# Delta-rule attention into a hard-swish MLP: the triangular substitution dealt out by shares, x's sums moved up one unit, the eleven-product form in four blocks

## The chip, the cores and the metric

One NeuronCore of a Trainium2 chip runs the whole program. The metric is device microseconds of one execution. The kernel before was timed three times: 685.58, 686.8 and 688.06 us, median 686.8 us. Line numbers below are those of the kernel before, which are also the ones in its profile.

## The reference, cut to what matters

```python
# q, k, v: (4, 8, 768, 48); beta: (4, 8, 768); w_in: (384, 2048); w_out: (2048, 384); all float32
k_n = k / (norm(k, axis=-1) + 1e-06)
for t in range(S):                      # a 48x48 state for each of the 4*8 (batch, head) pairs
    y[:, :, t] = einsum('bhd,bhde->bhe', q[:, :, t], state)
    v_old = einsum('bhde,bhd->bhe', state, k_n[:, :, t])
    state = state + beta[:, :, t] * einsum('bhd,bhe->bhde', k_n[:, :, t], v[:, :, t] - v_old)
x = y.transpose(0, 2, 1, 3).reshape(3072, 384)
h = x @ w_in
g = h * clip(h + 3, 0, 6) / 6
out = g @ w_out
```

## The kernel before, in words

**Attention.** The 768 tokens are cut into 24 steps of 32 tokens; a step holds the 4 batches on 4 x 32 partitions. Within a step the token-by-token recurrence is replaced by a unit lower-triangular system of 32 x 32 for each of the 32 (batch, head) pairs. Its inverse X is made ahead of time for a group of four steps at once, 128 problems on 128 partitions, by forward substitution on VectorE (`inverse`). That is one transposing move in (L456), then 30 rounds of a multiply (L746, `pr<-A`) and a subtract (L751, `A<-A,pr`) on 30 to 240 elements a partition, a memset (L755) and one transposing move out (L460). Group 0 is step 0, group g holds steps 4g-3 to 4g, and the last has three. `norms` makes the inverse lengths of a group's keys, two groups ahead: a square `sq<-kf` (L398) and a sum over it (L400) for each step, through one scratch tile.

`chain(t)` is the serial part of a step: the state times K and Q (L793, `ks`), two pairs of operations that build the right side R (L806, `R<-ks`), X times R (L814, `pz`), the state's update (L912 `su`, L928) and the output y (L806, L814 `py`, L849). Its last piece turns y on TensorE (L859, `yt`) and copies it into the MLP's input xT (L863). `prep(t)` makes what depends on K and Q alone, some steps ahead; GpSimd scales keys and masks for it (L497, L473, L485).

**MLP.** Two steps make a block of 256 rows, 12 blocks in all. `up(blk)` multiplies by w_in: 16 units, each with three matmuls of 128x128 by 256 columns into one buffer `ph` of the PSUM pool `psM`. That pool has four buffers, and `pt`, `py`, `pz`, `yt` and the down products take turns in the same ring. ScalarE (L976) and then VectorE (L979, `g<-g,ph`) evict each unit. For the last two blocks `up_by_eleven(blk)` does the same with 11 products of 128x128x128 in place of 12 for each of 8 pairs of columns of w_in (L1039). It needs sums of w_in's parts, made once on GpSimd (`weight_sums`, L1005), four differences of x's parts on VectorE (`token_sums`, L1029), three additions on GpSimd for each pair (L1005, `g<-g`), and three operations each on ScalarE (L1053, L1076, L1080) and VectorE (L1069, L1070, L1083) for each pair. `down_by_seven(blk)` multiplies by w_out with seven products in place of eight, with sums of g's parts (L1182) and of the outputs (L1206) on VectorE; its matmuls are L1196.

**Order.** Nothing is left to a scheduler. The first steps follow a list of words written by hand. From step 5 on, a loop deals every step out over 15 units. Each unit issues what `plan` has for it (pieces of `chain` and `prep`, loads), then one unit of the MLP (`units`, which runs through down and up of each block), then the evictions that are due, and last some of `fill`. `fill` is `norms` at first and then `inverse` of the next group; whatever is left of it is drained when the next group begins, since X is needed there. A block's `up` begins in unit 12 of an odd step and ends in unit 12 of the next, and `down_by_seven` takes the units up to unit 11 of the odd step after. The amount of `fill` in a unit, and where the sums of x stand, are in these lines:

```python
UF = 10                                                   # first block by eleven products
12: lambda: token_sums(t // CB) if t % CB and t // CB >= UF else None,
if i == 1 == ready[0] and 5 < u < 12:
    continue
take(fill, 1 if mode["slow"] else 2 + (u % 3 == 0))
```

`mode["slow"]` is set while `up_by_eleven` runs. In groups 3 to 5 the substitution for the next group begins in unit 6 of the group's second step, pauses to unit 11, and then goes at 3, 2 and 2 operations a unit.

Of the kernel before, what the change touches and what calls it, by code (L numbers as in the profile page):

```python
# [14 lines left out]
ACTF = mybir.ActivationFunctionType  # L15
# [31 lines left out]
def kernel(  # L47
# [21 lines left out]
    nc = tc.nc  # L69
# [321 lines left out]
    def norms(g, i0, n):  # L391

        kf = kfs[g]
        ss = small.tile([P, n, H], FP32, name="ss")
        for i in range(n):
            needs(("k", first(g) + i0 + i))
            sq = work.tile([P, H, D], FP32, name="sq", bufs=1)
            nc.scalar.activation(out=sq[:], in_=kf[:, i0 + i], func=ACTF.Square)  # L398
            yield 1
            nc.vector.tensor_reduce(out=ss[:, i, :], in_=sq[:], axis=AX.X, op=ALU.add)  # L400
            yield

        root = small.tile([P, n, H], FP32, name="root")
        nc.scalar.activation(out=root[:], in_=ss[:], func=ACTF.Sqrt, bias=tiny, scale=0.25)
        yield
        t = small.tile([P, n, H], FP32, name="nt")
        nc.vector.reciprocal(out=t[:], in_=root[:])
        yield
        nc.vector.scalar_tensor_tensor(
            out=t[:], in0=ss[:], scalar=0.25, in1=t[:], op0=ALU.mult, op1=ALU.mult  # L410
        )
        yield
        nc.vector.scalar_tensor_tensor(
            out=t[:], in0=t[:], scalar=1e-6, in1=root[:], op0=ALU.add, op1=ALU.add
        )
        yield
        inv = small.tile([P, n, H], FP32, name="inv", bufs=4)
        nc.vector.reciprocal(out=inv[:], in_=t[:])
        for i in range(n):
            invs[first(g) + i0 + i] = inv[:, i, :]  # L420
        yield
# [516 lines left out]
            yield  # L938


    mode = {"slow": False}
    gs, pos, evicts = {}, {}, []
    relus, pending = ({name: [] for name in ("a", "b", "u")} for _ in range(2))

# [45 lines left out]
                past.add(("up", blk))  # L990
            yield

    UF = 10
    S1, S2, S4 = (sums_in[:, i] for i in range(3))

    def w_tiles(s, i):
# [24 lines left out]
        return [x[:, s, i * P : i * P + P] for s in range(NKT) for i in range(CB)]  # L1021

    def token_sums(blk):
        needs(("seam", blk * CB), ("seam", blk * CB + 1), ("up", blk - 1))
        B11, B12, B21, B22, _, _ = (
            x.rearrange("p (a b) -> p a b", b=16) for x in x_tiles(blk)
        )
        for out, a, b in ((T1x, B12, B11), (T2x, B22, T1x), (B12, B22, B12), (T4x, B21, T2x)):
            nc.vector.tensor_tensor(out=out, in0=a, in1=b, op=ALU.subtract)  # L1029
        past.add(("sums", blk))  # L1030

    def up_by_eleven(blk):
        needs(("sums", blk))
        mode["slow"] = True
        B11, T3x, B21, B22, B31, B32 = x_tiles(blk)
        phs, ready = {}, {}

# [63 lines left out]
        for j in range(NPR):  # L1101
            end(j)
            go(j - 1)
            if j + 2 < NPR:
                yield
                begin(j + 2)
                go(j)
                yield
            else:
                go(j)  # L1110
                if j == NPR - 1:
                    go(j)
                    mode["slow"] = False
                yield

    def to_dram(t, o):
# [144 lines left out]
    def mlp_units():  # L1261


        u1 = up(1)
        for f in range(0, NFC, WF):
            for c in range(CB):
                down(0, c, f)
                yield
            for _ in range(WF):
                next(u1)  # L1270
                yield
        def downs(blk):
            if blk >= FIRST:
                yield from down_by_seven(blk)
                return
            for c in range(CB):
                for f in range(0, NFC, WF):
                    if c == 0:
                        needs(*(("read", ("ph", blk, f + i, None)) for i in range(2)))
                    down(blk, c, f)  # L1280
                    yield

        for blk in range(1, N // CB):
            sums = weight_sums() if blk == UF - 1 else iter(())
            for _ in downs(blk):
                next(sums, None)
                next(sums, None)
                yield
            if blk + 1 < N // CB:
                for n, _ in enumerate((up_by_eleven if blk + 1 >= UF else up)(blk + 1)):  # L1290
                    if blk + 1 == FIRST and n >= HF:
                        drain(rest)
                        if n % 2:
                            last_quarter(n - HF - 1)
                    yield
# [101 lines left out]
    with tc.manual_schedule():  # L1397
# [9 lines left out]
        units = gens["u"]  # L1407
        fill = inverse_of(2)
        loads = iter(())
        for t in range(LS, N):  # L1410
            g, i = group(t)
            ch = chain_of(t)
            behind = t - LS < LA - LE
            first_of = t + min(LA, LE + t - LS)
            now, more, later = (prep_of(first_of + n) for n in range(3))
            if not behind:
                more, later = (), more
            take(gens["v"], 4)
            if i == 0:
                drain(fill)  # L1420
                fill = norms_of(g + 2)
            if i == 2:
                loads = keys_of(g + 3)
            plan = {
                0: lambda: take(ch),
                1: lambda: (take(ch), take(now)),
                2: lambda: (take(now), take(gens["q"], 4)),
                3: lambda: take(ch),
                4: lambda: (take(ch), take(now)),
                5: lambda: take(now),  # L1430
                6: lambda: take(now),
                8: lambda: take(ch),
                9: lambda: take(ch, 2),
                11: lambda: take(ch),
                12: lambda: token_sums(t // CB) if t % CB and t // CB >= UF else None,
                13: lambda: take(later),
            }
            if behind:
                for u in (7, 8, 10, 11, 12, 13):
                    plan[u] = lambda ch=plan.get(u): (ch and u < 13 and ch(), take(more))  # L1440
                plan[14] = lambda: take(later)
            ready = (2, 0) if behind or i == 2 and t - LS == LA - LE else (1, 6)
            for u in range(NU):
                if u in plan:
                    plan[u]()
                take(loads, 2)
                if (i, u) == ready:
                    drain(fill)
                    fill = inverse_of(g + 1)
                    take(fill)  # L1450
                take(rest)
                take(gens["a"])
                take(units)
                settle(1)
                while evicts:
                    evicts.pop(0)()
                if i == 1 == ready[0] and 5 < u < 12:
                    continue
                take(fill, 1 if mode["slow"] else 2 + (u % 3 == 0))
            drain(ch)  # L1460
        for _ in units:
            settle(2)
# [30 lines left out]
```

## Time and profile before

| | |
|---|---|
| median of three runs | 686.8 us (685.58 to 688.06) |
| the profiled execution | 685.55 us, of which its span is 683.8 us |
| granted TensorE clock | 0.99 of full speed |
| TensorE busy | 647.7 us, 95% of the span |
| VectorE busy | 475.2 us, 69% |
| ScalarE, GpSimd busy | 253.3 us, 118.3 us |
| chain that ended last | TensorE 78%, VectorE 16%, issue 2%, ScalarE 2% |

The profile is one execution. Each matmul of float32 appears as two records, so 48 matmuls are 96 records. A row of the timeline reads: start in us from the span's start, the stretch in us, engine, line, operation, output and inputs, count, and in brackets how long the engine had stood idle and what ended that. Records overlap where an engine is pipelined, so a sum of durations is a little more than the time they take. In steps 9 to 16 a step takes about 26 us, in steps 17 to 21 about 24 us. The product with w_in of block 7 begins near 446 us, that of block 8 near 498, of block 9 near 546, of block 10 near 594 and of block 11 near 641.

### The profile page before, as it was taken

Reading aid. Unit: us, or ns where it says so; the run is one execution under the profiler, and the core shown is the slowest. Engines: PE = TensorE matmul, PEld = TensorE weight load, DVE = VectorE, ACT = ScalarE, POOL = GpSimd, SP = SyncE. Lnnn points to the kernel's source line nnn. Section 1 sums busy time; section 2 is a strip of 40 time slices with the busy share of each in tenths; the row PEclk is TensorE's granted clock in tenths of the full one; section 3 lists DMA queues with packets and bytes.
Section 4 is the critical chain, followed back from the end, with each engine's and each line's share of the span. In section 5 each row is a group of like instructions: output and inputs, shape, how many; then the busy total and the mean of one; then the engine's idle time right before and its main releaser. Section 6 shows DMA issues by size and latency. Waiting matters only on the chain.

```text
span 683.8 us, 25829 instructions
## 1 busy us (share of the span) xinstructions
PE 647.7 (95%) x11368; PEld 572.6 (84%) x11368; DVE 475.2 (69%) x1234; ACT 253.3 (37%) x503; POOL 118.3 (17%) x200
## 2 busy tenths in 40 slices
PE   2588989999999999999999999999999999999997
PEld 2468977776689989989988988978988989999997
DVE  5888867898556996746985746985546995457354
ACT  5986776423133133232133132132232132143250
POOL 6240232002311100100100101102000032040230
PEclk9997999999999999999999999999999999999999
DMA  7995435402040030041030030020020020100000
GB/s 182 246 215 132 99 88 130 80 4 45 23 86 14 3 72 2 3 89 19 2 71 2 3 71 2 2 61 2 3 47 2 3 48 2 28 11 2 25 1 23
DMA packets 88496, 33.23 MB, mean 49 GB/s; under 512 B 80160, under 2 KB 83232, under 8 KB 88384
## 3 DMA queue, kind: packets, MB, share of 16 engines
q1 hardware_dynamic: 88128, 31.29, 20.5%
q8 instruction: 89, 1.46, 0.9%
q10 hardware_dynamic: 256, 0.30, 0.2%
q14 instruction: 23, 0.19, 0.1%
HBM read 26.84 MB, written 4.72 MB: 46 GB/s over the span
## 4 chain that ended last, share of the span: by engine, by line
PE 78%; DVE 16%; issue 2%; ACT 2%; DMA 1%; SPq 0%; POOL 0%; DVEq 0%; ACTq 0%
PE ph L968 28%; PE po L1196 22%; PE ph L1039 6%; PE po L1131 4%; PE pt L513 3%; PE ks L793 3%; DVE g L1182 3%; PE py L814 3%; PE su L912 3%; PE pz L814 2%; DVE A L751 2%; DVE pr L746 2%; PE sc L534 2%; PE yt L859 1%; PE pi L671 1%
## 5 line engine op out<-in xcount | busy, mean ns | idle before, releaser
L968 PE MATMUL ph<-xT,w_in 128*128 128x256 f32 (+1 forms) x1056 | 227.4, 368 | 3.4 <-DVE g L979 2.8
L968 PEld LDWEIGHTS ph<-xT,w_in 128*128 128x128 f32 x1056 | 185.3, 194 | 27.7 <-DVE g L979 3.9
L976 ACT ACTIVATE g<-ph,halves 128x256 f32<-128x256 f32 (+1 forms) x176 | 79.1, 453 | 165.5 <-PE ph L968 163.4
L979 DVE SCALAR_TENSOR_TENSOR g<-g,ph 128x256 f32<-128x256 f32 (+1 forms) x176 | 68.1, 391 | 67.4 <-ACT g L976 67.2
L1196 PE MATMUL po<-w_out,g 128*128 128x192 f32 x640 | 112.1, 326 | 0.0
L1196 PEld LDWEIGHTS po<-w_out,g 128*128 128x128 f32 x640 | 104.7, 190 | 0.4
L1196 PE MATMUL po<-spare,g 128*128 128x192 f32 x480 | 86.7, 332 | 0.0
L1196 PEld LDWEIGHTS po<-spare,g 128*128 128x128 f32 x480 | 77.2, 190 | 1.8
L1182 DVE TENSOR_TENSOR g<-g 128x256 f32<-128x256 f32 x160 | 65.7, 459 | 3.3 <-PE po L1196 3.2
L473 POOL TENSOR_TENSOR mb<-beta_tok,mask 128x256 f32<-128x256 f32 x38 | 25.9, 702 | 236.8 <-DVE LB L545 236.8
L751 DVE TENSOR_TENSOR A<-A,pr 128x30 f32<-128x30 f32 (+9 forms) x150 | 53.7, 358 | 3.4
L746 DVE TENSOR_TENSOR pr<-A 128x30 f32<-128x30 f32 (+9 forms) x150 | 52.0, 347 | 3.1
L348 ACT ACTIVATE spare<-spare,places 128x768 uint16<-128x768 uint16 (+1 forms) x56 | 52.4, 940 | 2.9 <-DMA spare<-in_moe_w_in_dram 2.0
L1131 PE MATMUL po<-w_out,g 128*128 128x384 f32 x128 | 45.6, 493 | 0.0
L1203 ACT ACTIVATE o<-po 128x192 f32<-128x192 f32 x40 | 13.2, 330 | 82.4 <-PE po L1196 82.4
L521 ACT ACTIVATE KQ<-pt 128x512 f32<-128x512 f32 x48 | 28.1, 594 | 29.6 <-PE pt L513 29.2
L1039 PE MATMUL ph<-xT,w_in 128*128 128x128 f32 x224 | 34.2, 278 | 0.2
L497 POOL TENSOR_TENSOR kb<-kf,inv 128x384 f32<-128x384 f32 x24 | 22.3, 930 | 66.2 <-PE yt L859 35.6
L1131 PEld LDWEIGHTS po<-w_out,g 128*128 128x128 f32 x128 | 23.2, 190 | 12.4
L1005 POOL TENSOR_TENSOR g<-g 128x128 f32<-128x128 f32 x48 | 21.8, 455 | 67.8 <-ACT g L1053 65.3
L863 ACT ACTIVATE xT<-yt 128x384 f32<-128x384 f32 x24 | 11.7, 486 | 57.2 <-PE yt L859 57.2
L793 PEld LDWEIGHTS ks<-state,KQ 64*64 64x64 f32 x1472 | 24.8, 138 | 8.6 <-issue 7.7
(137 smaller groups left out, 779.7 us busy)
## 6 DMA issues: line engine op xcount, KB each, us to landing
kf<-in_k_dram SPq DMA_DIRECT2D x96, 48.0 KB, 2.7
qb<-in_q_dram SPq DMA_DIRECT2D x96, 48.0 KB, 2.9
vf<-in_v_dram SPq DMA_DIRECT2D x96, 48.0 KB, 2.1
out_dram<-o SPq DMA_DIRECT2D x92, 48.0 KB, 1.6
spare<-in_moe_w_in_dram SPq DMA_DIRECT2D x4, 768.0 KB, 7.6
w_out<-in_moe_w_in_dram SPq DMA_DIRECT2D x4, 768.0 KB, 7.1
w_out<-in_moe_w_out_dram SPq DMA_DIRECT2D x4, 768.0 KB, 6.6
spare<-in_moe_w_out_dram SPq DMA_DIRECT2D x4, 768.0 KB, 4.8
```

What stands on the lines that cost most here:

```text
L348: nc.scalar.activation(out=z, in_=z if n else d.bitcast(I16)[:, :, :, 3], func=func, bias=places[:, n : n + 1], scale=scale,)
L746: nc.vector.tensor_tensor(out=pv, in0=A[:, j + 1 :, j].unsqueeze(2).to_broadcast([n, w, j]), in1=A[:, j, 0:j].unsqueeze(1).to_broadcast([n ...
L751: nc.vector.tensor_tensor(out=A[:, j + 1 :, 0:j], in0=A[:, j + 1 :, 0:j], in1=pv, op=ALU.subtract)
L793: nc.tensor.matmul(ph[y][c, e, D * p : D * p + D], lhsT=KQ[r, p * B // 2 + b // 2, 2 * y : 2 * y + 2, :].rearrange("k y c -> k (y c)"), rh ...
L814: nc.tensor.matmul(ps[rows(place(b)), D * h : D * h + D], lhsT=m(h)[rows(b)], rhs=z[rows(b), D * h : D * h + D], start=True, stop=True, sk ...
L968: nc.tensor.matmul(ph[:, cols], lhsT=w_in[:, s, f * 128 : (f + 1) * 128], rhs=xT[:, s, cols], start=(s == 0), stop=(s == NKT - 1),)
L976: nc.scalar.activation(out=g, in_=ph, func=ACTF.Relu, bias=half, scale=1.0 / 6.0)
L979: nc.vector.scalar_tensor_tensor(out=g, in0=g, scalar=1.0, in1=ph, op0=ALU.min, op1=ALU.mult)
L1039: nc.tensor.matmul(ph[:, n], lhsT=w, rhs=x, start=start, stop=stop, skip_group_check=True)
L1131: nc.tensor.matmul(pos[c][:], lhsT=gs[blk, f // 2][:, f % 2, c * P : (c + 1) * P], rhs=w_out[:, f, :], start=(f == 0), stop=(f == NFC - 1),)
L1182: nc.vector.tensor_tensor(out=A(f, *out), in0=A(f, *a), in1=A(f, *b), op=op)
L1196: nc.tensor.matmul(ps[n][:], lhsT=A(f - f % 2, *a)[:, f % 2], rhs=b[:, f], start=(f == 0), stop=(f == HF - 1),)
```

## The change

Four edits. `UF` goes from 10 to 8, so that blocks 8 to 11 and not only 10 and 11 use `up_by_eleven`; `weight_sums` moves from block 9 to block 7 with it. `token_sums` moves from unit 12 to unit 11, right behind the chain's last piece and before that unit's part of the down product. The amount of `fill` while the substitution runs is no longer 3, 2, 2 a unit: what is left is divided by the units left in the group, and weighted by 0.9 beside `up`, 0.7 beside `up_by_eleven` and 1.25 beside `down`. The pause in the group's second step ends after unit 8, not 11. From group 4 on, the squares of `norms` are made by GpSimd and not by ScalarE.

```diff
@@ -395,7 +395,12 @@
         for i in range(n):
             needs(("k", first(g) + i0 + i))
             sq = work.tile([P, H, D], FP32, name="sq", bufs=1)
-            nc.scalar.activation(out=sq[:], in_=kf[:, i0 + i], func=ACTF.Square)
+            if g < 4:
+                nc.scalar.activation(out=sq[:], in_=kf[:, i0 + i], func=ACTF.Square)
+            else:
+                nc.gpsimd.tensor_tensor(
+                    out=sq[:], in0=kf[:, i0 + i], in1=kf[:, i0 + i], op=ALU.mult
+                )
             yield 1
             nc.vector.tensor_reduce(out=ss[:, i, :], in_=sq[:], axis=AX.X, op=ALU.add)
             yield
@@ -938,7 +943,7 @@
             yield
 
 
-    mode = {"slow": False}
+    mode = {"of": "down"}
     gs, pos, evicts = {}, {}, []
     relus, pending = ({name: [] for name in ("a", "b", "u")} for _ in range(2))
 
@@ -990,7 +995,7 @@
                 past.add(("up", blk))
             yield
 
-    UF = 10
+    UF = 8
     S1, S2, S4 = (sums_in[:, i] for i in range(3))
 
     def w_tiles(s, i):
@@ -1021,6 +1026,8 @@
         return [x[:, s, i * P : i * P + P] for s in range(NKT) for i in range(CB)]
 
     def token_sums(blk):
+        if blk < UF or ("seam", blk * CB + 1) not in past:
+            return
         needs(("seam", blk * CB), ("seam", blk * CB + 1), ("up", blk - 1))
         B11, B12, B21, B22, _, _ = (
             x.rearrange("p (a b) -> p a b", b=16) for x in x_tiles(blk)
@@ -1031,7 +1038,6 @@
 
     def up_by_eleven(blk):
         needs(("sums", blk))
-        mode["slow"] = True
         B11, T3x, B21, B22, B31, B32 = x_tiles(blk)
         phs, ready = {}, {}
 
@@ -1110,7 +1116,6 @@
                 go(j)
                 if j == NPR - 1:
                     go(j)
-                    mode["slow"] = False
                 yield
 
     def to_dram(t, o):
@@ -1281,12 +1286,14 @@
                     yield
 
         for blk in range(1, N // CB):
+            mode["of"] = "down"
             sums = weight_sums() if blk == UF - 1 else iter(())
             for _ in downs(blk):
                 next(sums, None)
                 next(sums, None)
                 yield
             if blk + 1 < N // CB:
+                mode["of"] = "eleven" if blk + 1 >= UF else "up"
                 for n, _ in enumerate((up_by_eleven if blk + 1 >= UF else up)(blk + 1)):
                     if blk + 1 == FIRST and n >= HF:
                         drain(rest)
@@ -1407,6 +1414,8 @@
         units = gens["u"]
         fill = inverse_of(2)
         loads = iter(())
+        left = due = 0
+        SHARE = {"up": 0.9, "eleven": 0.7, "down": 1.25}
         for t in range(LS, N):
             g, i = group(t)
             ch = chain_of(t)
@@ -1418,6 +1427,7 @@
             take(gens["v"], 4)
             if i == 0:
                 drain(fill)
+                left = 0
                 fill = norms_of(g + 2)
             if i == 2:
                 loads = keys_of(g + 3)
@@ -1431,8 +1441,7 @@
                 6: lambda: take(now),
                 8: lambda: take(ch),
                 9: lambda: take(ch, 2),
-                11: lambda: take(ch),
-                12: lambda: token_sums(t // CB) if t % CB and t // CB >= UF else None,
+                11: lambda: (take(ch), token_sums(t // CB)),
                 13: lambda: take(later),
             }
             if behind:
@@ -1448,15 +1457,21 @@
                     drain(fill)
                     fill = inverse_of(g + 1)
                     take(fill)
+                    left, due = 2 * (C - 2) + 2, 0.0
                 take(rest)
                 take(gens["a"])
                 take(units)
                 settle(1)
                 while evicts:
                     evicts.pop(0)()
-                if i == 1 == ready[0] and 5 < u < 12:
+                if i == 1 == ready[0] and 5 < u < 9:
                     continue
-                take(fill, 1 if mode["slow"] else 2 + (u % 3 == 0))
+                if not left:
+                    take(fill, 2)
+                    continue
+                due += SHARE[mode["of"]] * left / max((GS - i) * NU - u - 4, 1)
+                take(fill, int(due))
+                left, due = max(left - int(due), 0), due - int(due)
             drain(ch)
         for _ in units:
             settle(2)
```

## The prediction

> **What bounds the kernel now.** I read the page's busy times and slices first, then busy time by stretch, then the timeline where TensorE's matmuls start late.
>
> ```profile
> PE 647.7 (95%) x11368; PEld 572.6 (84%) x11368; DVE 475.2 (69%) x1234; ACT 253.3 (37%) x503; POOL 118.3 (17%) x200
> PE   2588989999999999999999999999999999999997
> DVE  5888867898556996746985746985546995457354
> ```
>
> TensorE is full from the ninth slice on. VectorE swings between 4 and 9 with a period of about six slices, the four steps of a group: its peaks are the substitution. So TensorE sets the time, and VectorE costs something only where a peak makes TensorE wait. I took the starts of all matmuls and looked for steps longer than the shape's usual one. From 200 us on, apart from 0.09 to 0.14 us whenever the kind of matmul changes, only these stand out: 1.00 us at 246.8, 0.32 at 339.8, 0.99 at 350.5, 0.31 at 443.6, 1.34 at 454.2, 0.91 at 594, 0.89 at 641. That is 5.8 us in all, the most that a better order can give there. The largest:
>
> ```profile
> 453.89 0.74 DVE L806 SCALAR_TENSOR_TENSOR R<-ks,parity,vf 128x192 f32<-128x192 f32 x2
> 454.55 0.73 DVE L806 SCALAR_TENSOR_TENSOR R<-ks,parity,R 128x192 f32<-128x192 f32 x2
> 455.19 0.41 DVE L979 SCALAR_TENSOR_TENSOR g<-g,ph 128x256 f32<-128x256 f32 x1
> 455.66 1.56 PE L968 MATMUL ph<-xT,w_in 128*128 128x256 f32 x6 [1.18 <-DVE g L979]
> ```
>
> The eviction `g` stands behind R, and R behind substitution operations: `ks` was done near 450.8 and R begins at 453.89. The two `pt` of a `prep` have taken two of the four buffers of the ring, so the next `ph` has to wait for that `g`. The stalls at 246.8 and 350.5 are alike; those at 339.8 and 443.6 are `yt` waiting for y. The last two are the sums of x:
>
> ```profile
> 594.08 0.35 DVE L1206 TENSOR_TENSOR o<-u,po 128x192 f32<-128x192 f32 x1 [1.06 <-PE po L1196]
> 594.36 0.28 DVE L1029 TENSOR_TENSOR beta_tok<-xT 128x128 f32<-128x128 f32 x1
> 594.79 0.46 PE L1039 MATMUL ph<-beta_tok,sums_in 128*128 128x128 f32 x2 [0.52 <-DVE beta_tok L1029]
> ```
>
> xT was written by 593.27, but the sums stand behind `o<-u,po`, which waits for the last down product.
>
> **Eleven products in blocks 8 and 9.** GpSimd's rows pace block 11's pairs, where hardly anything else runs; the ordinary product is read between two rows of TensorE:
>
> ```profile
> 652.07 1.53 POOL L1005 TENSOR_TENSOR g<-g 128x128 f32<-128x128 f32 x3 [0.93 <-ACT g L1053]
> 654.52 1.52 POOL L1005 TENSOR_TENSOR g<-g 128x128 f32<-128x128 f32 x3 [0.93 <-ACT g L1053]
> 656.98 1.53 POOL L1005 TENSOR_TENSOR g<-g 128x128 f32<-128x128 f32 x3 [0.93 <-ACT g L1053]
> 367.30 2.76 PE L968 MATMUL ph<-xT,w_in 128*128 128x256 f32 x12
> 369.90 2.76 PE L1196 MATMUL po<-w_out,g 128*128 128x192 f32 x16
> ```
>
> A pair takes (656.98 - 652.07)/2 = 2.455 us with eleven products. Twelve records, two units, take 369.90 - 367.30 = 2.60 us. So 0.145 us a pair, 8 pairs, two more blocks: -2.3 us on TensorE. `weight_sums` are the same 16 operations in an earlier block; GpSimd is busy 17% of the span and 4.2 of 24 us beside block 7's product, so I cost them at nothing. If they were late, block 8's first products would wait for them.
>
> **Sums of x a unit earlier.** In blocks 10 and 11 they then start right after xT, near 593.3, and the first is done before the second product of the pair wants it at about 594.1. Of 0.91 + 0.89 us I take back 1.6: -1.6. The `o` operations that move behind them have 7 us until ScalarE's L1080 (at 601.5) writes their tile again. In blocks 8 and 9 the sums are new.
>
> **Spreading the substitution.** In the built order I counted L746 and L751 between one step's y (L849) and the next. Groups 3 and 4 have 28 then 32 before (down, then up) and 32, 26 and 2 after. So six operations of about 0.38 us, 2.3 us of VectorE, leave the part beside `up`, where R and `g` were late by more than 1 us of their margin. Of 0.99 + 1.34 I expect 1.8 back. The part before y has four more, but they begin in unit 9 and not 12 and thin out toward y (2.5 a unit falling to 2.0, against 2.3), so y may be about 0.2 us earlier at each of the two `yt`: 0.4 back. Together -2.2; the bounds are -3.0 (all stalls gone) and 0 (they only move). Group 2 is the other way: 21 then 35 become 25 then 32, so y of step 7 is some 1.2 us later (four of 0.3). Its `yt` has no margin to speak of when VectorE is that full (the two stalls of 0.3 show it), and the 1.0 us at 246.8 shrinks a little: +0.5, between -1.0 and +1.2.
>
> **Squares on GpSimd.** At steps 5, 9 and 13 ScalarE squares and VectorE sums in turn, 1.14 us a round. GpSimd's `kb<-kf,inv` of the same 384 elements takes 0.83 to 1.0 us, so a round becomes about 1.5, but only two rounds instead of three precede R: R comes no later. ScalarE gets free for `KQ<-pt`, which was late at step 5, where TensorE lost 0.8 us before `sc` at 169.3: -0.5, between -0.8 and +0.5 (if GpSimd delays a `kb`).
>
> **Block 9: substitution beside eleven products.** This decides. Before, 27 operations of the last substitution stand beside block 9's product with w_in; after, 24, for the share of 0.7 takes out few when the deadline is near. The stretch before, and block 10 without substitution:
>
> ```profile
> core 0: us, PE busy (x) PEld busy (x) DVE busy (x) ACT busy (x) POOL busy (x), PEclk, DMA share, GB/s
> 546.00:570.00 24.00, 24.00 (x352) 20.55 (x351) 21.11 (x54) 7.97 (x17) 8.76 (x12) 1.00 0.16 36
> 594.00:618.00 24.00, 23.41 (x427) 22.49 (x426) 12.18 (x32) 11.46 (x23) 10.84 (x24) 1.00 0.11 26
> ```
>
> VectorE before: 21.1 us. Out go 16 `g` of 0.42 (6.7) and three substitution operations (about 1.2). In come 8 times 0.29 + 0.42 + 0.68 = 1.39 (11.1) and four sums of 0.29 (1.2): 25.5 us, against 24.0 - 1.2 = 22.8 of TensorE. It is over by 2.7. GpSimd adds to it:
>
> ```profile
> 439.14 1.03 POOL L485 TENSOR_TENSOR bkb<-kb,beta_tok 128x384 f32<-128x384 f32 x1 [3.46 <-PE su L912]
> 439.52 0.91 DVE L751 TENSOR_TENSOR A<-A,pr 128x234 f32<-128x234 f32 x1
> ```
>
> An `A<-A,pr` of this size takes 0.40 us elsewhere; it ends 0.3 us after GpSimd's. Six operations of VectorE are stretched so beside `weight_sums` between 551 and 561, 2.6 us in all, which the 21.1 contains; R and `g`, which read PSUM, are not stretched (0.73, 0.41 us). GpSimd now has 24 additions of 0.5 us, 12.1 for 8.8 us, so 2.6 may become 3.6: +1.0. And VectorE enters later, with four more operations beside block 8's down product (+1.4). The upper bound is 2.7 + 1.0 + 1.4 = 5.1 us. The lower is 0: VectorE may fall behind by a ring's depth, about one pair (2.5 us) or a little more, and catch up in the next down product, where it is busy 12.1 of 24 us. Before, that stretch lost nothing at 88% of VectorE. I take the middle, +2.7: about 1.2 of it where block 9's second product waits for the sums of x, the rest where a begun pair waits for a buffer. Block 8 has only five operations and the move in (1.97 us) beside its product: +0.3, between 0 and 1.
>
> The Trainium skill (SBUF — State Buffer, "Who interferes with whom") says that a VectorE instruction with two SBUF inputs and a GpSimd instruction that reads SBUF exclude each other, the second waiting until the first is done; the rows at 439 agree. By that rule alone, block 9's product would hold the port for 12.1 us of GpSimd, 8 of substitution, 5.5 of L1083 and 2 of other sums, 27.6 us for 22.8, so it speaks against the change: about +4.8 in place of +2.7, and about -1.0 for the whole.
>
> **Sum.** -2.3 - 1.6 - 2.2 + 0.5 - 0.5 + 2.7 + 0.3 = -3.1 us: the profiled 685.55 becomes 682.4. The median lies 1.25 above that execution, so the forecast is 686.8 - 3.1 = 683.7 us. A measurement of this kernel tells 0.3%, 2.1 us, from no change.
>
> **Rivals.** (a) Block 9 hides its load behind the ring as before: without the 2.7 and 0.3 the sum is -6.1, 680.7 us. For it: TensorE was at 24.00 of 24.00 us there. Against it: 25.5 us of VectorE in 22.8. (b) The spread only moves the stalls: VectorE has as much to do, and the later ends meet the next step's work. Then -2.2 becomes 0 and the sum is -0.9, 685.9, no change. For it: the operations beside `down` grow. (c) Slower. GpSimd and VectorE take turns in blocks 8 and 9: each substitution operation waits out a whole addition of 0.5 us, and GpSimd's delay holds up L1069 in turn. 24 + 5 operations times 0.5 are 14.5 us, of which some 4 fit into VectorE's idle time and 2.5 into the ring; with the 2.7 over and 1.4 late that is +12 in place of +3.0, so the sum is about +6, 692.8. It decides for slower once an operation waits more than 0.35 us on average ((3.1 + 2.1 us over what the forecast has) / 29 = 0.18, beside the 0.1 to 0.2 already in). Rows near 559 show 0.20 to 0.57 beside additions of 0.73, so half a wait of 0.5 is likelier. (d) The change not doing what it says: the built order shows all four edits, so only their effect is open.
>
> **How the numbers follow.** Forecast (681.8 to 685.5) 0.42, (a) 0.18, (b) 0.20, (c) in its whole width from +1.5 us 0.20. Faster by over 0.3% (below 684.7): 0.8 of the forecast's cases and all of (a), 0.52. Slower by over 0.3% (above 688.9): the upper two thirds of (c), 0.14, and 0.04 from unknowns, 0.18. Within: 0.30. The range leaves out the best part of (a) and the far part of (c): 680.3 to 689.0.
>
> **What would show it.** Right: no matmul of `ph` late by 1 us near 350 and 454; none behind the sums of x in blocks 10 and 11; blocks 8 and 9 with 2.455 us a pair where no chain piece lies between; a stall of 1 us or more at the start of block 9's product, with VectorE above 95% in it. Wrong: TensorE full through block 9 (then a), substitution rows of 0.7 us and more throughout block 9 with TensorE idle several us (then c), or `yt` and R late by as much as before (then b).

## The result and the profile after

The changed kernel takes 685.23 us (median of 20 runs, 681.46 to 689.79), the kernel before 688.0 us on the same chip (20 runs, 683.4 to 693.02). The ratio is 0.9958, 95% interval 0.9942 to 0.9974: about 2.8 us faster. The profiled execution after took 685.23 us with a span of 683.1. Line numbers after are those of before plus 5 to 7; a line is named here by its tiles too.

The page of after, busy times and two rows of slices:

```profile
PE 644.3 (94%) x11528; PEld 575.7 (84%) x11528; DVE 487.6 (71%) x1258; ACT 257.1 (38%) x508; POOL 150.3 (22%) x259
PE   2668989999999999999999999999999999999997
DVE  5878776888645996746986746987548998557364
```

TensorE has 3.4 us less to do and is still full from the ninth slice on. VectorE shows the same swing. Its last peak has nines in slices 32 and 33 as before, and the slices on both sides of them have gone from 6 and 5 to 8 and 8: blocks 8 and 9.

**Where the time went.** The first 155 us wait on loads and vary by themselves: the first `yt` of step 4 came at 154.39 us before, at 157.56 after, and between 153.9 and 158.9 in the runs below, whose instructions up to there do not differ. From then on a stretch whose instructions do not differ repeats to 0.05 us from profile to profile, with one exception: step 20 of the two versions below with an early last group, -0.38 and -0.57. For this reason all differences below are taken between first `yt` records in the trace: "step 7" runs from the first `yt` of step 6 to that of step 7, and "to the end" is the last matmul's end. There is one profile of each kernel. Each kernel against the kernel before, in us:

| steps | 5 | 7, 8 | 11, 12 | 15, 16 | 18, 19 | 20, 21 | 22 to the end | all from step 5 |
|---|---|---|---|---|---|---|---|---|
| the changed kernel | -0.30 | +0.83 | -1.29 | -1.64 | +0.12 | +0.42 | -2.10 | -3.96 |
| dealing-out alone | -0.51 | +0.82 | -1.29 | -1.64 | 0.00 | 0.00 | -0.01 | -2.65 |
| eleven in blocks 8, 9 alone | -0.02 | -0.02 | -0.02 | -0.02 | +0.31 | +4.24 | -0.01 | +4.46 |
| sums of x alone | -0.02 | -0.02 | -0.02 | -0.03 | 0.00 | 0.00 | -2.09 | -2.18 |
| squares on GpSimd alone | +0.49 | -0.03 | -0.02 | -0.38 | 0.00 | 0.00 | -0.01 | +0.07 |
| all but eleven in blocks 8, 9 | -0.33 | +0.80 | -1.29 | -1.63 | 0.00 | 0.00 | -2.10 | -4.55 |

**The stalls.** After 200 us four places of the changed kernel lose over 0.2 us: 1.10 us before `yt` at 240.6, 0.71 before `ph` at 251, 1.12 before `yt` at 545.3, and 0.86 with 0.30 before the sums' products at 548. Those of 0.3, 0.99, 0.3 and 1.34 us near 340, 350, 444 and 454 are gone, and none is left behind the sums in blocks 10 and 11. The timeline of after at the start of block 9's product (here and below, rows that do not bear on the reading are left out):

```profile
543.38 0.41 DVE L756 TENSOR_TENSOR A<-A,pr 128x240 f32<-128x240 f32 x1
543.71 1.01 DVE L933 TENSOR_TENSOR state<-state,su 128x384 f32<-128x384 f32 x2
544.63 0.55 DVE L854 TENSOR_TENSOR y<-y,py 128x384 f32<-128x384 f32 x1
545.33 0.52 PE L864 MATMUL yt<-ident,y 128*128 128x128 f32 x3 [0.96 <-DVE y L854]
545.88 0.49 ACT L868 ACTIVATE xT<-yt 128x384 f32<-128x384 f32 x1 [6.88 <-PE yt L864]
546.70 0.36 DVE L1211 TENSOR_TENSOR o<-o 128x192 f32<-128x192 f32 x1
...
547.41 0.40 DVE L756 TENSOR_TENSOR A<-A,pr 128x234 f32<-128x234 f32 x1
547.73 0.28 DVE L1036 TENSOR_TENSOR beta_tok<-xT 128x128 f32<-128x128 f32 x1
548.07 0.49 PE L1045 MATMUL ph<-beta_tok,sums_in 128*128 128x128 f32 x2 [0.70 <-DVE beta_tok L1036]
```

y stands behind substitution operations without a gap on VectorE, and TensorE waits for it. xT is written at 546.37, yet its first sum begins at 547.73: it waits its turn behind the last sums of the down product (`o`) and two more substitution operations. Block 10, with no substitution beside it, begins at once when xT is there:

```profile
594.61 0.29 DVE L1036 TENSOR_TENSOR beta_tok<-xT 128x128 f32<-128x128 f32 x1 [0.94 <-ACT xT L868]
```

Where R was late before, near 350 us, it stood behind substitution operations until 2.78 us after the first `ph` behind `ks` (at 347.04), and the `g` behind R held up the next `ph`:

```profile
349.82 0.73 DVE L806 SCALAR_TENSOR_TENSOR R<-ks,parity,vf 128x192 f32<-128x192 f32 x2
351.59 1.13 PE L968 MATMUL ph<-xT,w_in 128*128 128x256 f32 x4 [0.82 <-DVE g L979]
```

After, R begins 1.02 us behind that `ph`, its `g` is done in time, and the next `ph` does not wait:

```profile
350.53 1.56 PE L973 MATMUL ph<-xT,w_in 128*128 128x256 f32 x6
351.55 0.74 DVE L811 SCALAR_TENSOR_TENSOR R<-ks,parity,vf 128x192 f32<-128x192 f32 x2
352.85 0.41 DVE L984 SCALAR_TENSOR_TENSOR g<-g,ph 128x256 f32<-128x256 f32 x1
354.10 2.11 PE L973 MATMUL ph<-xT,w_in 128*128 128x256 f32 x9
```

### The profile page after: what moved, and what is told of

The parts are those of the page before. It is cut to its first block, busy times and chain, and to the rows that moved or that the text cites. A ratio compares the mean times of both kernels' runs of the same rounds, so it can differ in the third digit from the quotient of the medians.

```text
span 683.1 us, 26265 instructions
## 1 busy us (share of the span) xinstructions
PE 644.3 (94%) x11528; PEld 575.7 (84%) x11528; DVE 487.6 (71%) x1258; ACT 257.1 (38%) x508; POOL 150.3 (22%) x259
## 4 chain that ended last, share of the span: by engine, by line
PE 80%; DVE 12%; issue 3%; ACT 2%; DMA 1%; SPq 1%; POOL 1%; DVEq 0%; ACTq 0%; POOLq 0%
PE ph L973 23%; PE po L1201 23%; PE ph L1045 12%; PE po L1136 5%; PE ks L798 3%; PE pt L518 3%; PE py L819 3%; PE pz L819 3%; PE su L917 3%; PE sc L539 2%; DVE pr L751 2%; DVE A L756 2%; DVE g L1187 2%; ACT spare L348 1%; PE yt L864 1%
## 5 line engine op out<-in xcount | busy, mean ns | idle before, releaser
L973 PE MATMUL ph<-xT,w_in 128*128 128x256 f32 (+1 forms) x864 | 184.0, 365 | 2.1 <-ACT spare L348 1.3
L973 PEld LDWEIGHTS ph<-xT,w_in 128*128 128x128 f32 x864 | 149.8, 195 | 21.4 <-DVE g L984 1.5
L981 ACT ACTIVATE g<-ph,halves 128x256 f32<-128x256 f32 (+1 forms) x144 | 64.2, 449 | 130.4 <-PE ph L973 130.4
L1201 PEld LDWEIGHTS po<-w_out,g 128*128 128x128 f32 x640 | 104.5, 190 | 0.3
L984 DVE SCALAR_TENSOR_TENSOR g<-g,ph 128x256 f32<-128x256 f32 (+1 forms) x144 | 55.1, 386 | 51.8 <-ACT g L981 51.4
L1010 POOL TENSOR_TENSOR g<-g 128x128 f32<-128x128 f32 x96 | 44.6, 467 | 139.7 <-ACT g L1059 134.6
L1045 PE MATMUL ph<-xT,w_in 128*128 128x128 f32 x448 | 69.2, 278 | 0.1
L1045 PEld LDWEIGHTS ph<-xT,w_in 128*128 128x128 f32 x448 | 58.9, 192 | 0.9 <-issue 0.3
L1059 ACT ACTIVATE g<-ph 128x512 f32<-128x512 f32 x32 | 19.1, 596 | 40.2 <-PE ph L1045 32.0
```

The costliest lines, as they stand in the source:

```text
L973: nc.tensor.matmul(ph[:, cols], lhsT=w_in[:, s, f * 128 : (f + 1) * 128], rhs=xT[:, s, cols], start=(s == 0), stop=(s == NKT - 1),)
L981: nc.scalar.activation(out=g, in_=ph, func=ACTF.Relu, bias=half, scale=1.0 / 6.0)
L984: nc.vector.scalar_tensor_tensor(out=g, in0=g, scalar=1.0, in1=ph, op0=ALU.min, op1=ALU.mult)
L1010: nc.gpsimd.tensor_tensor(out=out, in0=a, in1=b, op=op)
L1045: nc.tensor.matmul(ph[:, n], lhsT=w, rhs=x, start=start, stop=stop, skip_group_check=True)
L1201: nc.tensor.matmul(ps[n][:], lhsT=A(f - f % 2, *a)[:, f % 2], rhs=b[:, f], start=(f == 0), stop=(f == HF - 1),)
```

## The experiments

The theory (A) is the prediction's: VectorE works through one queue, and TensorE loses what VectorE's order makes late for `yt`, R, `g` or the sums of x. The rivals: operations beside GpSimd cost double (the port), or VectorE has simply too much to do in steps 18 to 20 (the volume).

**The four edits one at a time.** First the dealing-out alone:

```diff
-    UF = 8
+    UF = 10
-                11: lambda: (take(ch), token_sums(t // CB)),
+                11: lambda: take(ch),
+                12: lambda: token_sums(t // CB) if t % CB and t // CB >= UF else None,
```

with the squares on ScalarE again.

> The dealing-out of the substitution alone (shares 0.9 and 1.25, pause to unit 8), with eleven products in blocks 10 and 11 only, sums of x in unit 12 and squares on ScalarE. Theory A, the parts add up and each acts where VectorE's volume of substitution lies: from one yt to the next, steps 12 and 16 are shorter by 1.1 and 1.45 us than before, steps 11 and 15 by 0.2 each, step 7 is 1.1 longer and step 8 0.3 shorter; steps 18 to 21 within 0.5 of before, since block 9's product is the ordinary one; from step 5 on -2 us in all. Rival B, these gains come from the squares on GpSimd or from blocks 8 and 9: steps 12 and 16 as before.

685.28 us, ratio 0.9968 (0.9947 to 0.999). Steps 11, 12, 15, 16 and 7, 8 are those of the changed kernel to 0.01 us, so they belong to this edit. So does step 5, -0.51, but not because R comes earlier: R does follow two key sums there and not three, yet `pz` begins 14.19 us after the `yt` before it with and without the edit. What TensorE waits for before `sc` is ScalarE's `y<-ks`, as in the kernel before:

```profile
170.11 0.86 PE L534 MATMUL sc<-KQ 64*32 64x64 f32 x64 [0.64 <-ACT y L830]
```

On ScalarE `KQ` stood between `root` and `y<-ks`, and with the new order it stands ahead of `root`, so `y<-ks` begins 0.48 us sooner.

The eleven products alone, `UF = 8` in the kernel before:

> Eleven products in blocks 8 to 11 alone, with the old dealing-out (3, 2, 2 operations a unit, 1 beside eleven products) and sums of x in unit 12. Theory A: block 8 and block 9 each give 1.0 us, each of their starts loses 0.9 us to late sums as in blocks 10 and 11 (step 18 and step 20), no yt(19) stall, and about 12 operations and the move out (about 5 us of VectorE) are drained as step 21 begins, of which 0 to 3 us reach TensorE; from step 5 on between 0 and +3 us. Rival C, GpSimd's port is what costs in block 9: additions and 16 operations beside them cost 2 us or more between yt(19) and yt(20) without any stall at the sums.

693.5 us (four runs), ratio 1.0113 (1.0094 to 1.0132), and +4.46 us in the trace, where 0 to +3 was expected. The timeline shows the sums of block 9 where unit 12 of the old order has them, with VectorE busy all through:

```profile
547.61 0.39 PE L1039 MATMUL ph<-xT,w_in 128*128 128x128 f32 x2
...
549.65 0.35 DVE L1206 TENSOR_TENSOR o<-u,po 128x192 f32<-128x192 f32 x1
550.36 0.40 DVE L746 TENSOR_TENSOR pr<-A 128x234 f32<-128x234 f32 x1
550.67 0.29 DVE L1029 TENSOR_TENSOR beta_tok<-xT 128x128 f32<-128x128 f32 x1
551.02 0.49 PE L1039 MATMUL ph<-beta_tok,sums_in 128*128 128x128 f32 x2 [3.03 <-DVE beta_tok L1029]
```

TensorE's next matmul starts 3.19 us late there, 3.03 us of it idle. That is not all: the windows from that wait on (time, PE, PEld, DVE, ACT, POOL busy, granted clock, DMA share, GB/s) show a second price.

```profile
core 0: us, PE busy (x) PEld busy (x) DVE busy (x) ACT busy (x) POOL busy (x), PEclk, DMA share, GB/s
547.85:551.00 3.15, 0.14 (x2) 0.00 (x0) 2.91 (x10) 0.00 (x0) 0.00 (x0) 1.00 0.08 23
551.00:552.10 1.10, 0.95 (x6) 0.79 (x7) 1.07 (x5) 0.00 (x0) 0.00 (x0) 1.00 0.42 112
552.10:555.60 3.50, 3.50 (x19) 3.50 (x19) 0.34 (x1) 1.19 (x2) 2.11 (x5) 0.51 0.42 96
555.60:560.00 4.40, 4.40 (x94) 4.22 (x94) 2.71 (x8) 1.36 (x3) 1.25 (x4) 1.00 0.15 28
```

For 3.5 us after the wait the granted clock is 0.51 and a matmul starts every 0.213 us in place of 0.112: another 1.7 us. In the changed kernel the same wait is 0.86 us. That the sums in unit 11 make this difference is likely but not shown by itself, since the substitution is dealt out differently there too.

The sums of x alone, in unit 11 of the kernel before:

> The sums of x right behind the output's turn, alone. Theory A: nothing changes before block 10; step 22 and the stretch from yt(23) to the end are shorter by 1.05 us each, -2.1 us in all, and no matmul waits for the sums. Rival B, the gain there comes from elsewhere (VectorE's work moved out of the way): less than 1 us.

685.7 us, ratio 0.9982 (0.9955 to 1.001), inconclusive by the clock; the trace has -1.05 us in each of the two blocks and nothing elsewhere.

The squares alone on GpSimd (a profile and one time, 687.87 us):

> The squares of groups 4 to 6 on GpSimd, alone. Theory A: step 5 is shorter by 0.3 us, as TensorE waits less for KQ before sc; steps 9 and 13 are as before; nothing else moves. Rival B: GpSimd's delay reaches a kb or VectorE's R and step 5 or 9 is longer by 0.5 us or more.

Step 5 is slower by 0.49; the 0.36 saved in step 16 the dealing-out has anyhow. Step 5 in this run, then in the changed kernel:

```profile
171.39 0.32 ACT L409 ACTIVATE root<-ss,places 128x32 f32<-128x32 f32 x1 [4.30 <-DVE ss L405]
171.62 0.58 ACT L526 ACTIVATE KQ<-pt 128x512 f32<-128x512 f32 x1
172.09 0.57 ACT L835 ACTIVATE y<-ks,parity 128x384 f32<-128x384 f32 x1
172.72 0.86 PE L539 MATMUL sc<-KQ 64*32 64x64 f32 x64 [1.14 <-ACT y L835]
```

```profile
169.28 0.60 ACT L526 ACTIVATE KQ<-pt 128x512 f32<-128x512 f32 x1 [1.13 <-PE pt L518]
172.13 0.32 ACT L409 ACTIVATE root<-ss,places 128x32 f32<-128x32 f32 x1 [2.26 <-DVE ss L405]
172.36 0.56 ACT L835 ACTIVATE y<-ks,parity 128x384 f32<-128x384 f32 x1
172.97 0.86 PE L539 MATMUL sc<-KQ 64*32 64x64 f32 x64 [0.34 <-ACT y L835]
```

A square takes 0.83 us in place of 0.52, and a round of square and sum 1.50 in place of 1.14, so the last sum comes later. ScalarE, free of the squares, is no help: `root<-ss` waits for that sum (ScalarE idles for 4.30 us), and `y<-ks`, for which `sc` waits, stands behind `root`. Counted from the `yt` before, `root` begins 0.49 us later than in the kernel before, which is the whole loss of step 5. Rival B has the size right, but neither a `kb` nor R is what came late: `pz` starts at 14.19 us here too. In the changed kernel `KQ` is indeed early, 3 us ahead of `sc`; `root` and with it `y<-ks` still come 0.19 us later than with the squares on ScalarE.

The other three together, without the eleven products in blocks 8 and 9 (the changed kernel with `UF = 10`; one time, 682.39 us):

> The changed kernel with eleven products in blocks 10 and 11 only, as before. Steps were additive so far: dealing-out alone gave -2.66 us from the output of step 5 to the end (the step before that included), the sums -2.19, the squares +0.13. Theory A: these add up, -4.6 to -4.9 us against the kernel before, where the changed kernel has -3.97; blocks 8 and 9 with eleven products cost 0.6 to 0.9 us more than they save. Rival: the sums and the dealing-out share a gain, and the sum is -4.0 or less.

-4.55 (last row of the table) against -4.76 for the three rows added, so the total adds up to about 0.2, a little short of theory A. In part that is luck: the squares cost 0.3 us less in step 5 than alone, and their gain in step 16 is contained in the dealing-out's. Against this run the eleven products in blocks 8 and 9 cost 0.59 us net in the changed kernel: 2.0 saved on TensorE, 2.55 lost.

**What costs the 2.55 us?** First the port. GpSimd's additions are left out in block 9 only:

```diff
-            plus_minus(gt[:, 1], gt[:, 1], gt[:, 2], ALU.add)
+            if blk != 9:
+                plus_minus(gt[:, 1], gt[:, 1], gt[:, 2], ALU.add)
```

and so for the other two.

> GpSimd's three additions a pair are left out in block 9 (that part of block 9's eleven products is not computed: its combination of sums is left out), so that GpSimd is nearly idle beside the last substitution. Everything else is the changed kernel. Theory A (VectorE's volume and the late entry of y set block 9's loss): the wait of 1.12 us before yt of step 19 and the two before the sums of x (0.86 and 0.30) stay within 0.2 us, and only the small waits go, so step 20 falls by 0.3 us or less. Rival P (the port shared with GpSimd sets it): the stretched operations fall back to 0.40 us, VectorE gains some 2 us, and the waits before the sums go as well: step 20 shorter by 1.0 us or more.

Steps 20, 21 go from +0.42 to +0.34, and the waits stay: 1.11 before `yt`, 0.86 and 0.29 before the sums. GpSimd's 24 additions cost 0.1 us, not several. Theory A has it. For the large waits the changed kernel's trace says the same without an experiment: GpSimd's first addition in block 9 begins at 550.09, behind the waits at 545 and 548, and GpSimd had been idle for 27.89 us until then.

```profile
550.09 3.23 POOL L1010 TENSOR_TENSOR g<-g 128x128 f32<-128x128 f32 x6 [27.89 <-ACT g L1059]
```

So in block 9 of the changed kernel the port is out.

Then the order. The last group's pause ends after unit 6 and its share becomes 1.7 up to unit 12 of that step, and 1.0 (0.95 beside the down product) behind it:

```diff
-                if i == 1 == ready[0] and 5 < u < 9:
+                early = g in (5,)
+                if i == 1 == ready[0] and 5 < u < (7 if early else 9):
...
+                if early and i == 1 and u < 13:
+                    share = 1.7
```

> The last group's substitution alone is dealt out earlier: some 12 operations move from block 8's down product and block 9's product to beside block 8's product with w_in, which has eleven products too. Theory A: VectorE is in time for y and for the sums of x in block 9, so the waits before yt of step 19 (1.12 us) and before the sums (1.16 together) go, block 8's product loses 0.5 us at most; 1.5 to 2.3 us less from the output of step 5 to the end than the changed kernel. Rival P (operations beside GpSimd's additions cost twice, wherever they stand): the loss only moves from block 9 to block 8, and the whole stays within 0.7 us of the changed kernel.

Only 0.45 us less than the changed kernel (684.96 us, one time). The waits before `yt` and before the sums are gone, as A said, but block 8 has a new one of 0.89 us, and the end of block 9's product another of 0.88:

```profile
518.28 0.24 DVE L756 TENSOR_TENSOR A<-A,pr 128x84 f32<-128x84 f32 x1
518.44 1.01 DVE L933 TENSOR_TENSOR state<-state,su 128x384 f32<-128x384 f32 x2
519.37 0.55 DVE L854 TENSOR_TENSOR y<-y,py 128x384 f32<-128x384 f32 x1
519.83 0.28 DVE L1075 TENSOR_TENSOR g<-ph,g 128x128 f32<-128x128 f32 x1
519.97 0.49 PE L1045 MATMUL ph<-xT,w_in 128*128 128x128 f32 x2 [0.72 <-DVE y L854]
```

Six early operations stand ahead of `state` and y. By the last row TensorE waits for y: the new pair takes the buffer of the ring that `py` holds until y has read it. In the changed kernel y is formed 1.4 us earlier in its step, and VectorE idles 0.84 us before the `g` behind it. So A's waits are right and its total is not, and P's total (within 0.7) is right without its mechanism: the six operations stand almost wholly where GpSimd is idle, and take 0.20 to 0.25 us each, no more than elsewhere.

The same with the second group dealt out evenly (1.0 beside the product, 1.05 beside the down product):

> As the run before it, and the substitution of the second group dealt out evenly (share 1.0 beside the product with w_in, 1.05 beside the down product, in place of 0.9 and 1.25). Theory A (y of step 7 came late because four operations stand behind the product with w_in): the wait of 1.10 us before yt of step 7 falls to 0.3 us or less, the wait before ph in step 8 stays below 1.0: 0.5 to 1.0 us less than the run before it. Rival: that wait is set by the operations that GpSimd stretches there (1.01 and 0.90 us for 0.4), and stays above 0.8 us.

The whole is 0.58 us less than the run before it (682.47 us, one time). Steps 7, 8 go from +0.80 to +0.41; the wait before `yt` falls to 0.22 us, as A said, but the one in step 8 grows from 0.70 to 1.18, above A's 1.0. The other 0.19 us lie in step 20, where the instructions are the same. The stretch by GpSimd has not gone, it has only met another operation, first the changed kernel, then this run:

```profile
234.90 1.11 POOL L490 TENSOR_TENSOR bkb<-kb,beta_tok 128x384 f32<-128x384 f32 x1 [3.34 <-PE su L917]
235.25 1.01 DVE L751 TENSOR_TENSOR pr<-A 128x220 f32<-128x220 f32 x1
235.98 0.97 POOL L502 TENSOR_TENSOR kb<-kf,inv 128x384 f32<-128x384 f32 x1
236.30 0.90 DVE L756 TENSOR_TENSOR A<-A,pr 128x220 f32<-128x220 f32 x1
```

```profile
233.37 2.02 DVE L1187 TENSOR_TENSOR g<-g 128x256 f32<-128x256 f32 x2
235.31 0.36 DVE L756 TENSOR_TENSOR A<-A,pr 128x210 f32<-128x210 f32 x1
```

So the wait before that `yt` comes from the order (A): the pair `g<-g`, 0.75 us elsewhere, takes the stretch with about the same loss of VectorE (1.3 us against 1.1), and y is almost in time.

**The versions that should win.** Two blocks with eleven products, squares on ScalarE, second group even:

> The changed kernel with eleven products in blocks 10 and 11 only, the squares back on ScalarE and the second group dealt out evenly. Theory A (the parts add up): -4.55 us from the output of step 5 to the end with the squares on GpSimd, -0.2 for the squares back, -0.4 for the second group: -5.1 us against the kernel before, within 0.3. Rival: the squares on GpSimd also free ScalarE for something later, and taking them back costs 0.3 or more.

-5.09 us from step 5 on; 682.59 us against 687.75, ratio 0.9923 (0.990 to 0.9946), as theory A says. It is the shortest version here from step 5 on, and has the lowest ratio; the intervals of the ratios overlap, so the order among the versions rests on the traces.

Four blocks, the same two edits, and an early part cut to 11 operations:

> Eleven products in four blocks, squares on ScalarE, second group even, and the last group's substitution dealt out with 11 operations beside block 8's product (8 of them before y of its step is formed) in place of 17, 24 beside its down product, 23 beside block 9's. Theory A (block 9 loses what VectorE comes late, and block 8 loses only where operations stand between R and y): the wait of 0.89 us at the end of block 8's product falls below 0.3, and those at the start of block 9 (1.12 and 1.16 us in the changed kernel) to 1.0 together or less: -5.2 to -6.3 us against the kernel before. Rival V (VectorE's volume from step 17 to 20 is over, whatever the order): the waits only change place and the sum stays within 0.3 of the version with two blocks sent along.

-3.71 us; 684.01 us, ratio 0.9939 (0.9917 to 0.996). A's total fails: block 8's wait grew to 1.93 us. Seven operations stand between the transposing move (2 us) and `state`, where the run with 17 early operations had six, and they take 2.00 us against 1.34, since the last two stand beside an addition of GpSimd (0.38 and 0.52 us in place of about 0.25). So here GpSimd does have a part in the wait, some 0.4 us; another 0.35 is that the move itself comes later in its step. Block 9's start is as A said: 0.43 and 0.30 before the sums, and 0.35 at its end. V's number fails too: the sum is 1.4 us behind the version with two blocks, not within 0.3.

Four blocks with the pause kept, and the extra operations right behind y:

> As the version with four blocks before it, but with the pause in the last group's substitution kept as in the changed kernel; the operations that are taken out of block 8's down product now stand right behind y (8 in place of 5 up to block 8's end, 24 in place of 28 in the down product up to block 9). Theory A (what stands on VectorE between R and y, or ahead of the next eviction, decides): block 8's product loses 0.2 us or less, the wait before yt of step 19 falls from 1.12 to 0.3 or less, and block 9 keeps 0.7 before the sums and some 0.4 at its end: 0.6 to 1.2 us less from the output of step 5 to the end than the version with two blocks. Rival V (the volume is over): the waits only move again, and it is no better than the version with two blocks.

-3.95 us; 683.99 us, ratio 0.9955 (0.9934 to 0.9977). A fails again, and V holds: `yt` of step 19 waits 1.81 us, not 0.3. I had set the shares by the operations beside the down product. What counts is all that stands between y of step 18 and y of step 19, and in the trace that is 33 operations here, 32 in the changed kernel and 32 in the version with two blocks: nothing was taken out.

The same with block 9 ordinary, without sums of x for it (the line that decides is shown; its product then reads parts of w_in that `weight_sums` has already replaced, so the output of that block is not the reference's):

```diff
-                for n, _ in enumerate((up_by_eleven if blk + 1 >= UF else up)(blk + 1)):
+                for n, _ in enumerate((up_by_eleven if blk + 1 >= UF and blk != 8 else up)(blk + 1)):
```

> The same, with block 9 ordinary again: eleven products in blocks 8, 10 and 11. Theory A (only block 9, where half of the last substitution stands beside the product, is over): all waits of block 9 vanish and block 8 keeps its gain of 1.0 us, so that it is about 1.0 us less than the version with two blocks from the output of step 5 to the end, and 0 to 0.4 less than the run before it. Rival V: block 8's own volume makes y of step 19 late again by 0.5 us or more, and half of the gain or more is lost.

-4.26 us; 684.57 us, ratio 0.9951 (0.9931 to 0.9971). It is 0.83 us behind the version with two blocks, where A had it 1.0 ahead. Block 9's waits vanish, but `yt` of step 19 waits 1.81 us as before:

```profile
541.03 0.55 DVE L854 TENSOR_TENSOR y<-y,py 128x384 f32<-128x384 f32 x1
541.72 0.52 PE L864 MATMUL yt<-ident,y 128*128 128x128 f32 x3 [1.65 <-DVE y L854]
```

This settles whose wait it is: block 8's, handed in a step later. The version with two blocks has y and `yt` like this:

```profile
543.85 0.55 DVE L854 TENSOR_TENSOR y<-y,py 128x384 f32<-128x384 f32 x1
...
545.91 0.49 PE L864 MATMUL yt<-ident,y 128*128 128x128 f32 x3
```

y is done at 544.40, 1.51 us ahead of `yt`. The changed kernel from one `yt` to the next over block 8's product, its down product and block 9's product (time, PE, PEld, DVE, ACT, POOL busy, granted clock, DMA share, GB/s):

```profile
497.40:519.73 22.33, 22.33 (x417) 21.73 (x415) 13.97 (x34) 9.97 (x20) 9.67 (x21) 1.00 0.18 38
519.73:545.33 25.60, 24.64 (x394) 23.46 (x392) 22.89 (x68) 6.49 (x15) 1.43 (x3) 1.00 0.01 2
545.33:569.09 23.76, 22.93 (x416) 21.97 (x416) 21.70 (x60) 10.09 (x20) 9.82 (x21) 1.00 0.17 36
```

From `yt` of step 18 to the end of y of step 19, the version with two blocks and then the changed kernel:

```profile
521.98:544.40 22.42, 22.42 (x367) 21.19 (x366) 19.72 (x60) 4.41 (x11) 0.00 (x0) 1.00 0.01 2
519.73:545.18 25.45, 24.64 (x393) 23.42 (x391) 22.74 (x68) 6.49 (x15) 1.43 (x3) 1.00 0.01 2
```

With eleven products `yt` of step 18 comes 1.54 us sooner, and the end of block 8 then stands behind it. TensorE has 0.54 us of that to do in step 19, so it gains 1.0 us over the block. VectorE has 3.0 us more to do before y of step 19 (22.74 against 19.72) and idles for 2.7 us in both: about 2.6 us more for the evictions of block 8's last pairs (3.8 us against 1.3), most of the rest substitution operations that stood ahead of `yt` before. So y comes 3.03 us later behind `yt`, and the next `yt` is wanted 0.54 us later. The margin is 1.51 less the 0.15 us that lie between y and `yt` even where TensorE waits. 3.03 - 0.54 - 1.36 = 1.13: the changed kernel has 1.12. In the last two versions y comes 26.14 us behind `yt`, 3.72 later: the same sum gives 1.82, and 1.81 was measured.

Over the versions with four blocks and the sums in unit 11, steps 18 to 21 lose 2.0 to 3.4 us (their difference plus the 2.0 saved). The best order tried, with 17 early operations, comes out at +0.14 and -0.04 us in its two runs, so it loses all of the 2.0 saved. Rival V holds in this sense: within the orders tried here no placing pays, though VectorE is busy 89% and 91% in steps 19 and 20, not full. That some finer order would pay is not excluded.

## Why the prediction was right, and where not

The forecast was -3.1 us, the medians say -2.8 (the interval of the ratio is -1.8 to -4.0) and the trace from step 5 on -3.96. (683.7 us was forecast and 685.23 measured mainly because the forecast started from a median of three, 686.8, where twenty runs have 688.0.) The order on VectorE was the right mechanism; the terms differ.

**Eleven products:** -2.3 predicted, -2.0 measured (each block -1.54 and +0.54). **Sums of x:** -1.6 against -2.1; I took back less than the whole of 0.91 and 0.89, and small delays of 0.06 to 0.10 us in each block (below the size that I looked for) go with them. **Groups 3 and 4:** -2.2 against -2.93, near the bound where all stalls go; both `yt` and both R are in time, so rival (b) is wrong. **Group 2:** +0.5 against +0.83. Its `yt` indeed had no margin: 1.10 us, of which the shrinking stall of step 8 gives back 0.27.

**Squares:** -0.5 predicted, the wrong sign: +0.2 in the changed kernel (step 5: -0.50 with the squares on ScalarE in the two-block version, -0.33 with them on GpSimd), +0.5 alone. The step that failed is "ScalarE gets free for `KQ`": I took the square off ScalarE's queue and forgot `root`, which stayed on it ahead of `y<-ks`, for which `sc` waits. With the squares alone it is ahead of `KQ` too; in the changed kernel the dealing-out has already put `KQ` ahead of it. `root` waits for the last sum, and the longer rounds, which I put at nothing, make that sum later.

**Left out:** the dealing-out by itself shortens step 5 by 0.51 us, for which the forecast has no term. So the -0.30 seen there is near the -0.5 forecast by luck: it is -0.5 of the dealing-out and +0.2 of the squares.

**Blocks 8 and 9:** +0.3 and +2.7 predicted, 2.55 us together measured: the sum of 3.0 is near, the split is wrong. Block 8 loses nothing beside its own product (22.33 us, as block 10), so I would have called the +0.3 too high; but 1.12 us of the loss, at `yt` of step 19, are its debt. I priced a block by what stands beside its product, and the wait is due where the next y is: 2.6 us of its evictions are behind `yt`. Block 9's own part is 1.16 us before the sums, for which I had written "about 1.2", and 0.3 of small ones, not the 1.5 at the ring. The sign "VectorE above 95%" did not come: it was 91% from `yt` to `yt`. VectorE was late, not full.

The rule of the Trainium skill (SBUF — State Buffer, "Who interferes with whom") fits the rows at 235 us, where operations of 0.4 us beside GpSimd's of 1 us take 1.01 and 0.90. As a price for block 9 (+4.8 by the rule alone) it was far off: taking GpSimd's additions away gave 0.1 us. Eleven operations in step 20 were stretched, by 0.1 to 0.2 us each and 1.7 us in all, and the large waits lie ahead of them. So rival (c) fails by its own mechanism; rival (a) fails on the waits at 545 and 548.

## What to carry to other kernels

A faster stage on the busiest engine brings forward every deadline behind it. Follow the work that it adds on the second engine to the next few deadlines: what falls between one deadline and the next comes out of the margin there, not only in the stage itself, and what falls where that engine idles costs nothing. When an operation is moved off an in-order engine, look at what else on that engine waits for its result, and read from the profile which of the operations there the busy engine waits for. And moving work within a full stretch trades one wait for another; take the edits one at a time before believing that the sum needs all of them, since here the version without the largest of them is the shortest in the traces.

## What was unexpected of the hardware

After TensorE had stood idle for 3.03 us (the matmul behind it 3.19 us late) its clock was granted at 1.00 for 1.1 us more and then at 0.51 for 3.5 us, which added 1.7 us to the wait; a wait of 1.93 us, 1.77 of it idle (1.00 granted in the 6 us after it) had no such price. The Trainium skill (TensorE: Matmul & The Clock Gate, "Part 1: The HAM clock gate") puts this at one idle window of about 3.4 us on a free-running clock; here a little less was enough. GpSimd stretched a pair of VectorE operations from 0.75 to 2.02 us beside two of its own of 0.87 and 1.01, yet 24 additions of about 0.5 us beside VectorE's substitution cost TensorE 0.1 us in all.
